# The last 64 query rows of all four experts scored as one TensorE group on four array quarters, with order and bank tables written anew

## The chip, the cores and the metric

The kernel runs on one core of a Trainium2 chip. The metric is the device time of one execution in microseconds (us). Five engines work side by side, each through its own queue in order: TensorE (PE in the profile, with PEld for its weight loads), VectorE (DVE), ScalarE (ACT), GpSimd (POOL) and SyncE (SP), which here only issues DMA transfers. Matrix products land in PSUM, which this kernel uses as eight banks of 128 partitions by 512 floats.

## The reference

Two stages follow one another for each of 8 batches of 576 rows. The first is attention with 8 heads of width 64 in which every score below (row maximum - tau) is dropped. Its output, 576 rows of 512, goes into the second stage: four experts, each a causal attention of its own with head width 64, weighted per row by a gate that keeps two of the four.

```python
scores = scale * np.matmul(q, k.transpose(0, 1, 3, 2))
scores = np.where(scores >= scores.max(-1, keepdims=True) - tau, scores, -1e9)
attn = softmax(scores); x = (attn @ v)                      # 8 batches, 8 heads, 576 x 64
...
w = softmax of the two largest of x @ w_gate
for e in range(4):                                          # second stage
    q, k, v = x @ wq[e], x @ wk[e], x @ wv[e]
    a = softmax(causal(scale * q @ k.T))
    out += w[:, :, e] * (a @ v @ wo[e])
```

## The kernel before

576 rows are four blocks of 128 and a tail of 64. The first stage takes heads in pairs (four pairs in a batch, 32 in all); the second stage takes experts in pairs (`ep` 0 and 1), the two experts `j` of a pair lying in partitions 0 to 63 and 64 to 127. `projected` makes the transposed queries and keys of a pair (tiles of the family `q2`, 128 x 576), `values` the value rows and the gate weights (`gw`, and `gt` for the tail rows). For a row block `t` of 0 to 3, `scores2` makes a score matrix per expert in a bank each, DVE adds the causal mask and takes a row minimum (L801), ACT takes the exponential with its row sum (L818), DVE inverts the sum (`inverse`: add epsilon L771, reciprocal L784), POOL multiplies by that and by the gate weight (L772). `transp2` turns the weights round on TensorE (L1355, small products with an identity, `ident`), `attnv2` multiplies by the values, and `output` by `wo` (6 products of 512 columns, `woh` and `wol`).

The tail (`t` = 4) has 64 rows for each expert, so the two experts of a pair fill one 128-partition tile together. Its scores are four products in float32: 64 query rows by 288 keys, twice, for each expert. They have a contraction of 64 and 64 result rows, so each uses one quarter of the 128 x 128 array: expert 0 the quarter (rows 0 to 63, columns 0 to 63), expert 1 the quarter (rows 64 to 127, columns 64 to 127). Both write the same bank, in different partitions. This group stands in the program twice in a batch, once for each pair. The first stage has a tail too, and scores two head pairs' tails in one group of eight such products (`kx`, `qz`): there all four quarters are in use.

The order is set by a planner (`Plan`): each step has a place (a number in the table `PLACE`, shifted by engine and tile in `PLACE_OP`), a TensorE group starts when its place comes and its tiles have room, and a table `BANKS` gives every PSUM tile its bank. `SLOTS` says how many buffers a family of tiles has. Where the planner foresees an idle TensorE in the first 160 us, `fill` puts in small products of a constant (`still`, L1352). Engines then run exactly the planned order, waiting only for data and for room.

Names in the rows: a printed name without its number is a family, so `q,q` is a product of `q2` tiles (64 x 288 is the tail, wider ones with 64*128 are the row blocks), `kx,qx` the first stage's scores, `T,vh` its products with values after a transposing DMA, `ident,p` the second stage's transposes, `pt,v` its products with values, `still` the filler. A float32 product counts as two instructions in the trace.

Of the kernel before, what the change touches and what calls it, by code (L numbers as in the profile page):

```python
# [28 lines left out]
         "x": 10, "v2": 1, "q2": 2, "zt": 2, "z0": 2, "z1": 2, "pt2": 5, "pa": 1, "pb": 2}  # L29
# [163 lines left out]
CHANGE = ((0, 160, 195, 115, 110, 160), (218, 23, 201, 119, 25, 150), (198, 163, 0, 20, 120, 163), (225, 165, 80, 0, 145, 165),  # L193
          (216, 25, 223, 150, 50, 150), (218, 150, 201, 119, 150, 23))
EXP_SB = True
AV2_GROUPS = ((4, 3), (2, 1, 0))
T2_GROUPS = ((4,), (3,), (2,), (1, 0))


# [1186 lines left out]
```

## Time and profile before

| what | value |
|---|---|
| median of 3 runs | 774.03 us (772.94 to 774.16) |
| the profiled execution | 773.78 us |
| its span, first to last instruction | 772.1 us |
| TensorE busy | 757.4 us, 98% |
| VectorE busy | 678.3 us, 88% |
| ScalarE busy | 659.3 us, 85% |
| GpSimd busy | 384.6 us, 50% |

The span leaves 1.7 us of the profiled time around it. Busy shares are averages; rows of the time line give start and length, and since TensorE's products overlap, the distance from one row's start to the next row's start is what a group really takes. The granted TensorE clock is full throughout.

### The profile page before, as it was taken

Reading aid. Unit: us, or ns where it says so; the run is one execution under the profiler, and the core shown is the slowest. Engines: PE = TensorE matmul, PEld = TensorE weight load, DVE = VectorE, ACT = ScalarE, POOL = GpSimd, SP = SyncE. Lnnn points to the kernel's source line nnn. Section 1 sums busy time; section 2 is a strip of 40 time slices with the busy share of each in tenths; the row PEclk is TensorE's granted clock in tenths of the full one; section 3 lists DMA queues with packets and bytes.
Section 4 is the critical chain, followed back from the end, with each engine's and each line's share of the span. In section 5 each row is a group of like instructions: output and inputs, shape, how many; then the busy total and the mean of one; then the engine's idle time right before and its main releaser. Section 6 shows DMA issues by size and latency. Waiting matters only on the chain.

```text
span 772.1 us, 27731 instructions
## 1 busy us (share of the span) xinstructions
PE 757.4 (98%) x10868; PEld 616.5 (80%) x10868; DVE 678.3 (88%) x2124; ACT 659.3 (85%) x1734; POOL 384.6 (50%) x547
## 2 busy tenths in 40 slices
PE   8999999999999999999999999999999999999998
PEld 6777878688777887788887887778876888778986
DVE  4899989988999889988999889998899988998374
ACT  5898879988899879988799987998899987998264
POOL 5776247543556246553475535663355633765010
PEclk9999999999999999999999999999999999999999
DMA  6541574955768577883768757696587758748002
GB/s 150 121 93 38 124 134 94 177 100 120 145 139 174 111 123 159 165 164 80 137 122 192 126 122 135 126 196 105 119 152 150 135 104 149 140 105 139 15 29 83
DMA packets 319058, 96.37 MB, mean 125 GB/s; under 512 B 305744, under 2 KB 314192, under 8 KB 318928
## 3 DMA queue, kind: packets, MB, share of 16 engines
q1 hardware_dynamic: 317584, 94.31, 61.8%
q8 instruction: 85, 1.39, 0.7%
q10 hardware_dynamic: 1344, 0.30, 0.2%
q14 instruction: 45, 0.37, 0.1%
HBM read 31.47 MB, written 9.44 MB: 53 GB/s over the span
## 4 chain that ended last, share of the span: by engine, by line
PE 68%; DVE 17%; ACT 6%; DMA 4%; issue 3%; POOL 1%; SPq 0%; ACTq 0%; DVEq 0%; POOLq 0%
PE banks L709 60%; PE banks L1355 8%; DVE pp L806 6%; DVE hl L795 3%; ACT pp L824 2%; ACT pp L818 2%; DVE col L772 2%; DMA T<-hl 2%; DMA ki<-in_k_dram 1%; DVE p L801 1%; DVE pa L746 1%; DVE st L746 1%; ACT p L818 1%; DVE x L795 1%; ACT pt L744 1%
## 5 line engine op out<-in xcount | busy, mean ns | idle before, releaser
L824 ACT ACTIVATE pp<-pp,col 128x576 f32<-128x576 f32 x284 | 209.7, 774 | 16.8 <-DVE col L784 6.1
L806 DVE TENSOR_SCALAR_CACHE_REDUCE pp<-banks 128x576 f32<-128x576 f32 x284 | 206.6, 749 | 11.7 <-PE banks L709 9.0
L772 POOL TENSOR_SCALAR hl<-pp,col 128x576 f16<-128x576 f32 x182 | 154.1, 859 | 125.9 <-DMA T<-hl 23.7
L818 ACT ACTIVATE pp<-pp 128x576 f32<-128x576 f32 x284 | 192.6, 682 | 0.1
L795 DVE SCALAR_TENSOR_TENSOR hl<-pp,col,hl 128x576 f16<-128x576 f32 x182 | 162.0, 896 | 3.3 <-POOL hl L772 3.2
L709 PE MATMUL banks<-kx,qx 64*128 64x288 f32 x1024 | 154.9, 421 | 0.9 <-ACT qz L742 0.4
L709 PEld LDWEIGHTS banks<-kx,qx 64*128 64x128 f32 x1024 | 92.3, 187 | 29.2 <-issue 6.4
L772 POOL TENSOR_SCALAR pp<-pp,col 128x576 f32<-128x576 f32 x102 | 77.2, 769 | 73.7 <-DVE col L784 37.3
L772 POOL TENSOR_SCALAR p<-p,col,gw 128x512 f32<-128x512 f32 (+3 forms) x115 | 81.1, 717 | 51.4 <-DVE col L784 40.5
L709 PEld LDWEIGHTS <-vh 128*64 128x64 f16 x2940 | 78.7, 110 | 9.5 <-issue 6.4
L709 PE MATMUL banks<-T,vh 128*64 128x128 f16 (+1 forms) x2940 | 85.1, 216 | 0.3 <-DMA T<-hl 0.2
L818 ACT ACTIVATE p<-p,col 128x512 f32<-128x512 f32 (+4 forms) x134 | 77.5, 585 | 8.3 <-DVE col L801 7.9
L801 DVE CUSTOM_DVE_ANT_0 p<-banks,mask 128x512 f32<-128x512 f32 (+4 forms) x134 | 64.3, 508 | 5.5 <-PE banks L709 5.3
L709 PE MATMUL banks<-q,q 64*64 64x288 f32 (+4 forms) x384 | 68.4, 448 | 0.1
L709 PE MATMUL banks<-wvh,x 128*128 128x260 f32 x320 | 62.5, 287 | 0.0
L744 ACT ACTIVATE pt<-banks 128x384 f32<-128x384 f32 (+2 forms) x128 | 57.6, 509 | 2.0 <-PE banks L1355 1.2
L818 ACT ACTIVATION_READ_ACCUMULATOR pp<-pp 128x1 f32 x284 | 56.7, 200 | 0.0
L709 PE MATMUL banks<-x,wqh 128*128 128x288 f32 x256 | 54.2, 304 | 0.0
L709 PEld LDWEIGHTS banks<-wvh,x 128*128 128x128 f32 x320 | 50.8, 188 | 3.8 <-issue 3.3
L709 PE MATMUL banks<-pt,v 128*64 128x128 f32 (+1 forms) x960 | 51.8, 259 | 0.4 <-ACT pt L744 0.3
L709 PE MATMUL banks<-x,wkh 128*128 128x288 f32 x256 | 52.0, 297 | 0.0
L709 PEld LDWEIGHTS banks<-pt,v 128*64 128x64 f32 x960 | 43.8, 137 | 7.3 <-issue 3.4
(141 smaller groups left out, 1553.6 us busy)
## 6 DMA issues: line engine op xcount, KB each, us to landing
ki<-in_k_dram SPq DMA_DIRECT2D x32, 256.0 KB, 3.7
vz<-in_v_dram SPq DMA_DIRECT2D x32, 256.0 KB, 2.9
qi<-in_q_dram SPq DMA_DIRECT2D x62, 128.0 KB, 2.8
out_dram<-st SPq DMA_DIRECT2D x30, 256.0 KB, 2.4
tk<-in_k_dram SPq DMA_DIRECT2D x14, 128.0 KB, 3.6
T<-hl SPq DMA_TRANSPOSE x91, 5.2
vz<-in_v_dram SPq DMA_DIRECT2D x64, 16.0 KB, 2.5
out_dram<-st SPq DMA_DIRECT2D x8, 128.0 KB, 3.3
```

Of the source, the lines that this page charges most:

```text
L709: lambda o, x, y: nc.tensor.matmul(o, x, y, start=start, stop=stop))
L744: run(e, t, [dst], [src], lambda d, s: nc.scalar.activation(d, s, AF.Copy))
L746: run(e, t, [dst], [src], lambda d, s: nc.vector.tensor_copy(d, s))
L772: return m.tensor_scalar(d, s, x_, y_, op0=op0, op1=op1)
L795: return nc.vector.scalar_tensor_tensor(d, a_, x_, r.pop(0), op0=op0, op1=op1, **kw)
L801: lambda o, a, i, m: nc.vector.tensor_tensor_reduce(o, i, m, 1.0, 3e38, ALU.add, ALU.min, a))
L806: lambda o, a, i: nc.vector.tensor_scalar(o, i, 1.0, None, op0=ALU.mult, op1=ALU.min, accum_out=a))
L818: return nc.scalar.activation(d, s, AF.Exp, scale=scale, **kw)
L824: lambda d, s, x: nc.scalar.activation(d, s, AF.Prelu, bias=x, scale=-1.0, alpha=1e36))
L1355: o.fn(*(r.place() for r in (*o.outs, *o.ins)))
```

## The change

1. `scores2` no longer handles the tail. A new `scores2_tails` scores both pairs' tails in one TensorE group of eight products. Pair 0 keeps its quarters; pair 1 is written crosswise: the product from rows 0 to 63 goes to columns 64 to 127 and the other way round. Each pair has two banks, so the group holds four.
2. Both pairs' row sums lie side by side in one small tile and are inverted by one add and one reciprocal.
3. `attnv2_tails` makes the value products of both pairs into one bank; one ACT copy and one DVE subtraction of 128 x 128 replace two each of 128 x 64.
4. Since pair 0's tail is now scored after pair 1's projections, its 64 query columns are copied by POOL into a small tile `qt`, and `q2` has three buffers in place of two.
5. `gt` is gathered crosswise. The filler constant shares its tile with `ones`.
6. `PLACE` (511 of 659 numbers), `PLACE_OP` and `BANKS` are written anew, so the order of all engines differs in many places.

```diff
-    "DVE v2": -170.4688, "DVE vh": 56.17593, "DVE warm": 30.05958, "DVE x": 53.23876, "DVE z0": 1.422731,
+    "DVE v2": -141.0707, "DVE vh": 51.88485, "DVE warm": -1.567455, "DVE x": 20.39441,
...
-         "x": 10, "v2": 1, "q2": 2, "zt": 2, "z0": 2, "z1": 2, "pt2": 5, "pa": 1, "pb": 2}
+         "x": 10, "v2": 1, "q2": 3, "zt": 2, "z0": 2, "z1": 2, "pt2": 5, "pa": 1, "pb": 2}
...
-AV2_GROUPS = ((4, 3), (2, 1, 0))
-T2_GROUPS = ((4,), (3,), (2,), (1, 0))
+AV2_GROUPS = ((3,), (2, 1, 0))
+T2_GROUPS = ((3,), (2,), (1, 0))
...
+            if not i and not ep:
+                qt = plan.tile("qt", [P, ST], F32)
+                copy("POOL", qt, t[:, SM:])
             res.append(t)
-        return res
+        return [*res, res[0][:, SM:] if ep else qt]
...
-            w = S
-            g = plan.tile("s", [P, 2, 512], F32)
-            for hf in range(2):
-                cols = slice(hf * HS, (hf + 1) * HS)
-                for rows in heads:
-                    matmul(g[rows, hf, :HS], q2[0][rows, SM:], q2[1][rows, cols], True, True, 2)
-            views = [g[:, :, :HS]]
...
+    def scores2_tails(b, q2, gates, base, pre):
+        plan.place = (base, f"{pre}s04")
+        nmx, sm = (plan.tile("col", [P, 2], F32) for _ in range(2))
+        gs = [plan.tile("s", [P, 2, 512], F32) for _ in range(EP)]
+        gs[1].v.first = gs[0].v
+        for hf in range(2):
+            cols = slice(hf * HS, (hf + 1) * HS)
+            for ep, g in enumerate(gs):
+                for j, rows in enumerate(heads):
+                    matmul(g[heads[j ^ ep], hf, :HS], q2[ep][2][rows], q2[ep][1][rows, cols], True, True)
+        p2 = []
+        for ep, g in enumerate(gs):
+            plan.place = (base, f"{pre}s{ep}4")
+            p2.append(plan.tile(("p2", "pp") if last[0] else "p2", [P, 2 * SM], F32))
+            e = halves(p2[ep][:, :S])
+            masked_min(e, g[:, :, :HS], halves(mask2), nmx[:, ep:ep + 1])
+            exp(e, e, bias=nmx[:, ep:ep + 1], accum=sm[:, ep:ep + 1], scale=-1.0)
+        inverse(sm)
+        pt = []
+        for ep, p in enumerate(p2):
+            plan.place = (base, f"{pre}s{ep}4")
+            scaled("DVE" if last[0] else "POOL", p[:, :S], p[:, :S], sm[:, ep:ep + 1], gates[1][:, ep:ep + 1], ALU.mult, ALU.mult)
...
+    def attnv2_tails(b, pt, v2, zh, zl, cols):
+        g = gbank()
+        for ep in range(EP):
+            for c in range(R + 1):
+                for j in range(2):
+                    o = c * P + (j ^ ep) * ST
+                    es = slice((2 * ep + j) * D, (2 * ep + j + 1) * D)
+                    matmul(g[heads[j], ep * ST:(ep + 1) * ST], v2[:, c, es], pt[ep][:, o:o + ST], c == 0, c == R)
+        gv = g[:, :EP * ST].rearrange("p (e c) -> p e c", e=EP)
+        copy("ACT", zh[:, :, cols], gv)
+        minus("DVE", zl[:, :, cols], gv, zh[:, :, cols].bitcast(F32))
...
+                pt = scores2_tails(b, q2, (gw, gt), base, pre)
+                if b % 2 == 0:
+                    ends[:] = [plan.tile("zt", [P, EP, P], F32R) for _ in range(2)]
+                plan.place = (base, f"{pre}a4")
+                attnv2_tails(b, pt, v2, *ends, heads[b % 2])
```

TensorE, third batch, before: pair 0's tail group (64x288 x4) ends a run of the next keys' transposes and is followed by the output of a row block.

```order
L1355 MATMUL banks<-ident,ki_61 128x64 x6
L1355 MATMUL banks<-ident,tk_86 128x64
L1355 MATMUL banks<-ident,ki_61 128x64
L709 MATMUL banks<-q_101,q_100 64x288 x4
L709 MATMUL banks<-woh,z_104 128x512
L709 MATMUL banks<-wol,z_104 128x512
```

TensorE, same batch, before: pair 1's tail group stands shortly behind the last of its projections (`x,wq`).

```order
L709 MATMUL banks<-x_94,wqh 128x288
L709 MATMUL banks<-x_93,wql 128x288
L1355 MATMUL banks<-ident,p_76 128x64 x16
L709 MATMUL banks<-kx_65,qx_63 128x288 x4
L709 MATMUL banks<-q_101,q_100 64x288 x4
```

TensorE, same batch, after: the one group of both pairs, between two outputs.

```order
L710 MATMUL banks<-wol,z_107 128x512
L710 MATMUL banks<-woh,z_108 128x512
L710 MATMUL banks<-q_100,qt_186 64x288 x2
L710 MATMUL banks<-q_101,q_102 64x288 x2
L710 MATMUL banks<-q_100,qt_186 64x288 x2
L710 MATMUL banks<-q_101,q_102 64x288 x2
L710 MATMUL banks<-woh,z_107 128x512
L710 MATMUL banks<-wol,z_107 128x512
```

Eight products stand together where four stood twice. Behind the group follow that output (six products of 512 columns), one first-stage score group (`kx,qx` 128x288 x4) and ten transposes of the next keys.

TensorE, same batch, after, right behind these: from the last of the keys' transposes to the first transposes of a tail result (`p_77`, x10).

```order
L1374 MATMUL banks<-ident,tk_85 128x64
L1374 MATMUL banks<-ident,ki_61 128x64
L710 MATMUL banks<-pt_110,v_99 64x128 x6
L710 MATMUL banks<-pt_112,v_99 64x128 x6
L710 MATMUL banks<-q_101,q_102 128x512 x2
L710 MATMUL banks<-kx_66,qx_64 128x288 x4
L1374 MATMUL banks<-ident,p_77 128x64 x10
```

Before, an output, two first-stage score groups, twelve transposes (`ident,p_76`) and one row block's scores (`q,q` 128x512 x2) stood between pair 0's group and its transposes (`ident,p_78`, x10).

POOL, third batch, before: the scaling of pair 0's tail (`p_78` with `gt`) behind two row blocks of the second stage and ahead of first-stage scalings (`hl`).

```order
L748 TENSOR_SCALAR gt_184<-gw_182 64x2 x2
L772 TENSOR_SCALAR p_76<-p_76,col_129,gw_182 128x384 x2
L772 TENSOR_SCALAR p_77<-p_77,col_119,gw_182 128x128 x2
L772 TENSOR_SCALAR p_78<-p_78,col_136,gt_184 128x576
L772 TENSOR_SCALAR hl_79<-pp_68,col_137 128x576 x2
```

POOL, same batch, after: both tails' scalings, with the same small tile `col_124` and a first-stage pair between them.

```order
L773 TENSOR_SCALAR hl_81<-pp_70,col_152 128x576 x2
L773 TENSOR_SCALAR p_77<-p_77,col_124,gt_184 128x576
L773 TENSOR_SCALAR pp_69<-pp_69,col_120 128x576 x2
L773 TENSOR_SCALAR p_76<-p_76,col_124,gt_184 128x576
L773 TENSOR_SCALAR hl_79<-pp_68,col_141 128x576 x2
```

The two tails stood nine rows apart on POOL and now stand two apart.

TensorE, last batch, after: the group stands one row of transposes behind pair 1's last key projection (`x,wk`).

```order
L710 MATMUL banks<-x_94,wkh 128x288
L710 MATMUL banks<-x_93,wkl 128x288
L1374 MATMUL banks<-ident,p_77 128x64 x12
L710 MATMUL banks<-q_100,qt_186 64x288 x2
L710 MATMUL banks<-q_102,q_101 64x288 x2
```

In the other seven batches several microseconds of TensorE work stand between them. Counted over the whole order, TensorE goes from one kind of product to another (kinds by array shape, with transposes and half-precision products apart) 531 times before and 537 times after, and has 148 fillers before and 142 after.

## Rows read from the trace of the kernel before

**Rows 1.** Page, part 1: busy us, share, instructions.

```profile
PE 757.4 (98%) x10868; PEld 616.5 (80%) x10868; DVE 678.3 (88%) x2124; ACT 659.3 (85%) x1734; POOL 384.6 (50%) x547
```

**Rows 2.** Windows: length, then busy PE, PEld, DVE, ACT, POOL, clock, DMA.

```profile
109.00:155.00 46.00, 44.88 (x668) 33.55 (x666) 44.16 (x148) 45.19 (x117) 30.31 (x39) 1.00 0.79 143
155.00:740.00 585.00, 581.64 (x8500) 475.33 (x8495) 526.59 (x1657) 512.16 (x1356) 290.84 (x397) 1.00 0.67 131
```

**Rows 3.** Windows for the filler's line alone: PE, PEld, clock, DMA.

```profile
109.00:155.00 46.00, 5.49 (x37) 2.96 (x37) 1.00 0.79 143
```

**Rows 4.** Groups of TensorE products, shapes apart: count, busy us, mean ns, idle before.

```profile
L709 PE MATMUL banks<-kx,qz 64*64 64x288 f32 x256 | 19.3, 415 | 0.0
L709 PE MATMUL banks<-q,q 64*64 64x288 f32 x128 | 19.0, 415 | 0.0
```

**Rows 5.** Time line of TensorE around pair 0's tail group, third batch: start, length.

```profile
288.12 0.35 PE L1355 MATMUL banks<-ident,ki 64*128 64x64 f32 x6
...
288.31 0.22 PE L1355 MATMUL banks<-ident,ki 64*128 64x64 f32 x1
288.47 1.19 PE L709 MATMUL banks<-q,q 64*64 64x288 f32 x8
289.59 0.50 PE L709 MATMUL banks<-woh,z 128*128 128x512 f32 x1
```

**Rows 6.** Time line of TensorE around a first-stage tail group on four quarters.

```profile
227.74 1.20 PE L709 MATMUL banks<-kx,qz 64*64 64x288 f32 x16
228.87 0.28 PE L709 MATMUL banks<-col,ones 128*64 128x1 f32 x4
229.08 0.50 PE L709 MATMUL banks<-woh,z 128*128 128x512 f32 x1
...
230.67 1.24 PE L709 MATMUL banks<-kx,qx 64*128 64x288 f32 x8
231.84 0.50 PE L709 MATMUL banks<-woh,z 128*128 128x512 f32 x1
```

**Rows 7.** Time line, all engines: the way of that tail from exponential to transposes.

```profile
290.88 0.77 ACT L818 ACTIVATE p<-p,col 128x576 f32<-128x576 f32 x1
291.55 0.20 ACT L818 ACTIVATION_READ_ACCUMULATOR p<-p,col 128x1 f32 x1
291.88 2.17 POOL L772 TENSOR_SCALAR p<-p,col,gw 128x384 f32<-128x384 f32 x4
292.07 0.17 DVE L784 RECIPROCAL col<-col 128x1 f32<-128x1 f32 x1
293.95 1.13 PE L709 MATMUL banks<-q,q 64*128 64x512 f32 x4
294.02 0.83 POOL L772 TENSOR_SCALAR p<-p,col,gt 128x576 f32<-128x576 f32 x1
294.91 0.52 PE L1355 MATMUL banks<-ident,p 64*128 64x64 f32 x10
```

**Rows 8.** Time line of TensorE, last batch: value products of 128 columns.

```profile
755.87 2.84 PE L709 MATMUL banks<-pt,v 128*64 128x128 f32 x48
```

**Rows 9.** Time line, last batch: last product of a projection and its copy.

```profile
746.32 0.29 PE L709 MATMUL banks<-x,wql 128*128 128x288 f32 x1
746.71 0.41 ACT L744 ACTIVATE q<-banks 128x288 f32<-128x288 f32 x1 [1.25 <-PE banks L709]
```

**Rows 10.** Groups of DVE and POOL instructions that the change adds or removes.

```profile
L755 DVE TENSOR_TENSOR zt<-banks,zt 128x64 fp32r<-128x64 f32 x16 | 3.4, 212 | 1.4 <-ACT zt L744 1.2
L755 DVE TENSOR_TENSOR z<-banks,z 128x128 fp32r<-128x128 f32 x16 | 4.5, 284 | 3.1 <-ACT z L744 3.1
L784 DVE RECIPROCAL col<-col 128x1 f32<-128x1 f32 x16 | 2.5, 156 | 0.2
L772 POOL TENSOR_SCALAR p<-p,col,gw 128x128 f32<-128x128 f32 x28 | 13.0, 473 | 5.7 <-ACT zt L744 3.0 <-ACT x L742 1.6 <-DVE col L772 1.0
```

**Rows 11.** Waits: POOL for a reciprocal; total us, times, longest.

```profile
POOL hl L772 <- DVE col L784: 20.5, 13, 2.7
```

More of the change, by code (lines that the diff above doesn't have):

```diff
@@ L160 @@
-    "ACT wqh": -8.614884, "ACT wvh": -61.59402, "ACT x": 51.80171, "ACT z0": 13.77228, "ACT z1": 21.38886,
-    "ACT zt": 75.06289, "DVE col": -65.78447, "DVE gate": -58.83315, "DVE gt": 50.60351, "DVE gw": -85.47739,
-    "DVE hl": 114.5464, "DVE kx": -5.703491, "DVE lg": 91.45051, "DVE p2": -17.02737, "DVE pa": 5.055651,
-    "DVE pp": 1.799467, "DVE qsc": 151.7334, "DVE st": 9.31911, "DVE still": -70.95507, "DVE tau_p": -59.16886,
-    "DVE v2": -170.4688, "DVE vh": 56.17593, "DVE warm": 30.05958, "DVE x": 53.23876, "DVE z0": 1.422731,
@@ L170 @@
-    "POOL woh": 39.26528, "POOL wol": 61.43774, "POOL wqh": 90.91714, "POOL wql": -33.05171, "POOL wvh": -25.50643,
-    "POOL wvl": -100.8319, "SP T": -284.0837, "SP ki": -32.54941, "SP lg": -23.16328, "SP out": -197.8732,
-    "SP qi": 0.244049, "SP st": -150.7584, "SP tk": 9.732419, "SP tq": -143.6642, "SP vz0": -34.81607,
-    "SP vz1": -20.35572,
+    "ACT gw": -162.6874, "ACT kx": 108.3985, "ACT lg": 32.86921, "ACT p2": -218.0769, "ACT pb": -180.7968,
+    "ACT pp": 93.41855, "ACT pt2": -44.22563, "ACT q2": -81.22372, "ACT q2d0": -19.04289, "ACT q2d1": -63.05565,
@@ new lines @@
+    "ACT qi": 97.04683, "ACT qx": -46.61529, "ACT qz0": -36.58193, "ACT qz1": -122.443, "ACT tau_t": 22.37296,
+    "ACT tq": 88.41551, "ACT v2": 14.9347, "ACT warm": 82.36406, "ACT wkh": 33.61568, "ACT woh": -31.10502,
+    "ACT wqh": -8.614884, "ACT wvh": -61.59402, "ACT x": 66.07489, "ACT z0": 71.76126, "ACT z1": 35.58804,
+    "ACT zt": 67.6444, "DVE col": -83.97126, "DVE gate": -92.70674, "DVE gt": 104.5688, "DVE gw": -39.35556,
+    "DVE hl": 136.2087, "DVE kx": 3.353303, "DVE lg": 91.45051, "DVE ones": 31.69671, "DVE p2": 5.73354,
@@ new lines @@
+    "DVE pa": 8.331859, "DVE pp": 7.85189, "DVE qsc": 77.806, "DVE st": 5.74597, "DVE still": -44.37944,
+    "DVE tau_p": -47.34204, "DVE v2": -141.0707, "DVE vh": 51.88485, "DVE warm": -1.567455, "DVE x": 20.39441,
+    "DVE z0": 6.209092, "DVE z1": 44.79113, "DVE zt": 21.07184, "POOL col": -52.95213, "POOL gate": 27.92703,
+    "POOL gt": -49.52221, "POOL gw": 18.22398, "POOL hl": 107.7234, "POOL ident": 34.97707, "POOL mask": 185.7308,
+    "POOL mask2": -70.88285, "POOL ones": -68.97509, "POOL p2": 22.65193, "POOL pp": -67.71528, "POOL q2d0": 82.12945,
@@ new lines @@
+    "POOL q2d1": -277.5747, "POOL qt": -40.16381, "POOL qz0": -58.87586, "POOL qz1": -44.37684, "POOL st": 46.66943,
+    "POOL tie": -21.55509, "POOL v2": 2.057049, "POOL vh": -69.38473, "POOL vz0": 60.40645, "POOL vz1": -49.95888,
+    "POOL wkh": -62.83705, "POOL wkl": 10.16045, "POOL woh": 63.31141, "POOL wol": 62.66516, "POOL wqh": 70.22473,
+    "POOL wql": -18.89272, "POOL wvh": 14.14287, "POOL wvl": -96.68153, "SP T": -235.5178, "SP ki": -2.032985,
+    "SP lg": -17.05672, "SP out": -200.5112, "SP qi": 11.85062, "SP st": -168.3793, "SP tk": -44.33728,
@@ L849 @@
     qsc = const("qsc", [P, 1])
-    still = const("still", [P, P], BF16)
-    memset("DVE", still, 1.0)
+    ones = const("ones", [P, D])
+    memset("DVE", ones, 1.0)
+    still = ones.bitcast(BF16)
     memset("DVE", warm, 0.0)
@@ L873 @@
         memset("POOL", t[:, 2 * R * D:], 0.0)
-    memset("POOL", ones, 1.0)
     heads = [slice(j * D, (j + 1) * D) for j in range(2)]
@@ L1198, in values @@
         gt = plan.tile("gt", [P, EP], F32)
-        for j in range(2):
-            copy(soft, gt[j * ST:(j + 1) * ST], gw[ST:, R, j::2])
+        copy(soft, gt[:ST], gw[ST:, R, ::E - 1])
+        copy(soft, gt[ST:], gw[ST:, R, 1:E - 1])
         return v2, gw, gt
@@ L1205, in scores2 @@
         nmx, sm = (plan.tile("col", [P, 2], F32) for _ in range(2))
-        if t < R:
-            w = (t + 1) * P
-            gs = [gbank()[:, :w] for _ in range(2)]
-            gs[1].v.first = gs[0].v
-            for g, rows in zip(gs, heads):
-                matmul(g, q2[0][rows, t * P:w], q2[1][rows, :w], True, True)
-            views = gs
-        else:
-            w = S
-            g = plan.tile("s", [P, 2, 512], F32)
-            for hf in range(2):
-                cols = slice(hf * HS, (hf + 1) * HS)
-                for rows in heads:
-                    matmul(g[rows, hf, :HS], q2[0][rows, SM:], q2[1][rows, cols], True, True, 2)
-            views = [g[:, :, :HS]]
+        w = (t + 1) * P
+        views = [gbank()[:, :w] for _ in range(2)]
+        views[1].v.first = views[0].v
+        for g, rows in zip(views, heads):
+            matmul(g, q2[0][rows, t * P:w], q2[1][rows, :w], True, True)
         p2 = plan.tile(("p2", "pp") if last[0] else "p2", [P, 2 * SM], F32)
         for j, sv in enumerate(views):
-            e = p2[:, j * SM:j * SM + w] if t < R else halves(p2[:, :S])
-            masked_min(e, sv, mask[:, SM - w:] if t < R else halves(mask2), nmx[:, j:j + 1])
+            e = p2[:, j * SM:j * SM + w]
+            masked_min(e, sv, mask[:, SM - w:], nmx[:, j:j + 1])
             exp(e, e, bias=nmx[:, j:j + 1], accum=sm[:, j:j + 1], scale=-1.0)
-        nj = len(views)
         gw, gt = gates
-        inverse(sm[:, :nj])
-        gg = gw[:, t, 2 * ep:2 * ep + 2] if t < R else gt[:, ep:ep + 1]
-        for j in range(nj):
+        inverse(sm)
+        gg = gw[:, t, 2 * ep:2 * ep + 2]
+        for j in range(2):
             p = p2[:, j * SM:j * SM + w]
@@ L1233, in scores2 @@
         return p2
+    def scores2_tails(b, q2, gates, base, pre):
[15 more added lines that the diff above has]
+            exp(e, e, bias=nmx[:, ep:ep + 1], accum=sm[:, ep:ep + 1], scale=-1.0)
+        inverse(sm)
+        pt = []
+        for ep, p in enumerate(p2):
+            plan.place = (base, f"{pre}s{ep}4")
+            scaled("DVE" if last[0] else "POOL", p[:, :S], p[:, :S], sm[:, ep:ep + 1], gates[1][:, ep:ep + 1], ALU.mult, ALU.mult)
+            plan.place = (base, f"{pre}t{ep}4")
+            blocks = [(p[:, c * P:(c + 1) * P],) * 2 for c in range(R)] + [(p[:, S - P:S],) * 2]
+            pt.append(blocks_out(blocks, plan.tile("pt2", [P, len(blocks) * P], F32)))
+        return pt
+    def attnv2_tails(b, pt, v2, zh, zl, cols):
+        g = gbank()
+        for ep in range(EP):
+            for c in range(R + 1):
+                for j in range(2):
+                    o = c * P + (j ^ ep) * ST
[4 more added lines that the diff above has]
+        minus("DVE", zl[:, :, cols], gv, zh[:, :, cols].bitcast(F32))
     def transp2(tiles, p2, base, name):
@@ L1257, in attnv2 @@
                     es = slice((2 * ep + j) * D, (2 * ep + j + 1) * D)
-                    if t < R:
-                        x = pts[:, (j * (t + 1) + c) * P:(j * (t + 1) + c + 1) * P]
-                    else:
-                        x = pts[:, c * P + j * ST:c * P + (j + 1) * ST]
+                    x = pts[:, (j * (t + 1) + c) * P:(j * (t + 1) + c + 1) * P]
                     matmul(g[j * D:(j + 1) * D, o:o + m], v2[:, c, es], x, c == 0, c == t)
             o += m
-        a = 0
-        while a < o:
-            zh, zl, cols = z[tiles[0] if a == 0 else R - 1]
-            m = cols.stop - cols.start
-            copy("ACT", zh[:, ep, cols], g[:, a:a + m])
-            minus("DVE", zl[:, ep, cols], g[:, a:a + m], zh[:, ep, cols].bitcast(F32))
-            a += m
+        zh, zl, cols = z[tiles[0]]
+        copy("ACT", zh[:, ep, cols], g[:, :o])
+        minus("DVE", zl[:, ep, cols], g[:, :o], zh[:, ep, cols].bitcast(F32))
     def output(b, t, zh, zl, cols):
@@ L1292 @@
     family("gt", EP, 2)
+    family("qt", ST, 1)
     ends = []
@@ L1303, in moe @@
         v2, gw, gt = values(b, base, pre, parts)
-        tiles = (4, 3, 2, 1, 0)
+        tiles = (3, 2, 1, 0)
         for ep in range(EP):
@@ L1307, in moe @@
                 q2[1] = projected(b, 1, base, pre)
+                pt = scores2_tails(b, q2, (gw, gt), base, pre)
[3 more added lines that the diff above has]
+                attnv2_tails(b, pt, v2, *ends, heads[b % 2])
+                if b % 2:
+                    plan.place = (base, f"{'LM' if b == B - 2 else pre}o{R}")
+                    output(b, R, *ends, slice(0, P))
             pts, p2 = {}, {}
@@ L1317, in moe @@
                     if ep == 0:
-                        for x in ts:
-                            if x == R:
-                                if b % 2 == 0:
-                                    ends[:] = [plan.tile("zt", [P, EP, P], F32R) for _ in range(2)]
-                                z[x] = *ends, heads[b % 2]
-                            elif x == ts[0] or x == R - 1:
-                                zs = [plan.tile(f"z{k_}", [P, EP, words[f"z{k_}"] // EP], F32R) for _ in range(2)]
-                                z[x] = *zs, slice(0, words[f"z{k_}"] // EP)
+                        zs = [plan.tile(f"z{k_}", [P, EP, words[f"z{k_}"] // EP], F32R) for _ in range(2)]
+                        z[ts[0]] = *zs, slice(0, words[f"z{k_}"] // EP)
                     plan.place = (base, f"{pre}a{ep}{k_}")
```

48 lines of the change are left out of this document (16 added, 32 removed), and 236 rows, old and new, of the table PLACE.

## The prediction

> **What bounds the kernel now.** The first view is the page's busy shares: TensorE 98%, DVE 88%, ACT 85%, POOL 50% [rows 1]. An average over a long run can hide stages with other limits, so the second view is the table of windows [rows 2]. From 155 to 740 us, more than six of the eight batches, TensorE is busy for 581.64 of 585 us while DVE has 58 us free and ACT 73: there the time is the sum of what TensorE does, and a microsecond taken out of its work is a microsecond off the end unless a wait takes its place. Ahead of it, from 109 to 155 us, where the first batch's second stage starts, DVE and ACT are as full as TensorE (44.16 and 45.19 of 46 us), and 37 of TensorE's instructions are fillers [rows 3]: TensorE waits there, and less work for it is worth little. The third view is the time line, in which one reads the distance from start to start, since lengths of neighbouring rows overlap.
>
> **What the change takes from TensorE.** The trace holds both forms of a tail group. Sixteen second-stage groups on two quarters cost 19.0 us together, that is 1.19 us each; sixteen first-stage groups with twice the products on four quarters cost 19.3 us, 1.21 us each [rows 4]. So eight products on four quarters take as long as four on two. From start to start the first is 288.47 to 289.59 = 1.12 us [rows 5] and the second 227.74 to 228.87 = 1.13 us [rows 6]. The change runs 8 groups where 16 stood: 8 x 1.12 = **-8.96 us**. The group that is left is taken at 1.13 as before; crosswise quarters with two banks for each pair are not in the trace in just this form, and if they did not overlap the group would take 2 x 1.12 and nothing would be gained. I take the lower end because the four quarters themselves, in another pairing with banks, are there at 1.13.
>
> A page speaks against this. The rows: in the group of rows 5 both halves of the array's rows write one bank, in different partitions, and four products take 1.12 us, no more than four first-stage products that write two separate banks (230.67 to 231.84 = 1.17 us) [rows 6]. The Trainium skill, "TensorEngine Tiling (Array Packing)", Gotcha 1: PSUM Pressure, says that different row tiles cannot access the same bank at the same time. By that rule the group of rows 5 should take about double; the trace disagrees. In the changed group each pair's bank is again written from both row halves, so by the rule the sum would be 0 instead of -8.96; it is the second rival below.
>
> **Switches.** Going from one kind of product to another costs time of its own. In rows 5 six transposes take 288.12 to 288.31, 0.03 us each, but the last one's start lies 0.16 us ahead of the group's: about 0.13 us for the switch. The order after has 537 switches for 531. The distance of 1.12 us already holds the switch out of a group, so of the 8 removed groups 8 switches are paid for and 14 more come in elsewhere. Many of those are between transposes and other products with 64 rows, of which I have no clean row, so a price between 0 and 0.13 us: 0 to 1.8 us; I take 0.05, **+0.7 us**.
>
> **First and last batch.** In the first batch the group that goes away stands among fillers [rows 3], so most of its 1.12 us is not won. What DVE and ACT lose there counts instead, and it is small. DVE gives up two 212 ns subtractions for one of 284, and two reciprocals of 156 ns with the adds ahead of them for one of each [rows 10]: 0.14 + 0.3 = about 0.4 us a batch. That leaves **+0.7 us** of the 1.12 to be given back (between 0 and 1.1). In the last batch the group stands 12 transposes behind pair 1's last key projection. Such a projection ended at 746.61 and its ACT copy at 747.12, 0.51 us later [rows 9]; 12 transposes at 0.03 are about 0.4: **+0.1 us** once. In the other batches microseconds stand between, before as after.
>
> **Costed at nothing.** The saved ACT and DVE work in the other batches: both have over 50 us free there [rows 2]. The `qt` copy on POOL, 128 x 64: a 128 x 128 scaling took 473 ns [rows 10], so at most 0.5 us a batch on an engine that is half idle; if POOL were late already, it would cost the same 0.5 x 7 = 3.5 us. Four banks at once for the group: the first stage's tail group holds as many and shows no idle time ahead of it [rows 4]. The third `q2` buffer can only bring projections forward. SP's output transfers of the tail rows move with their group; SP waits for data, not data for it.
>
> **The wait that is added.** Both tails' sums go through one reciprocal, so the first tail's scaling on POOL now waits for the second tail's exponential. Behind it in POOL's queue stand a first-stage scaling pair, the second tail and a further `hl` pair whose transposing DMA feeds TensorE. Before, the way was: group over at 289.59, exponential at 290.88 (0.77 + 0.20 us), reciprocal done at 292.24, but POOL at the other scalings from 291.88 and at this one from 294.02 to 294.85; TensorE began its transposes at 294.91 without idling [rows 5, 7]. So 5.26 us from group to scaled tile, with 5.32 us of TensorE work in between: no slack to speak of. After, one exponential more: 5.26 + 0.97 = 6.23 us. The work in between is now an output (229.08 to 230.67 = 1.59), two score groups (2 x 1.17) [rows 6], the keys' transposes (about 0.4) [rows 5], 12 value products, 24 instructions (2.84 / 2 = 1.42 less the overlap, 1.4) [rows 8], and one row block's scores (293.95 to 294.91 = 0.96) [rows 7]: 6.7 us. So 0.47 us to spare: **0 us**, from 0 to what the rivals say.
>
> **Sum.** -8.96 + 0.7 + 0.7 + 0.1 = -7.46 us on the profiled execution's own 773.78 us gives 766.3; the median of the runs shown lies 0.25 us higher, so **766.6 us**.
>
> **Rivals.** *First, POOL late in part.* All places are new, and in the new order the first-stage scalings that stand ahead of the first tail on POOL themselves wait for reciprocals: such waits were 20.5 us in 13 times, 1.58 us in the mean, 2.7 at the longest [rows 11]. A mean wait in half of seven batches makes 6.23 + 1.58 - 6.7 = 1.1 us x 3.5 = 3.9 us: 770.5 us. For it: before had no slack at all. Against it: TensorE idled only 3.4 us in 585 [rows 2], so such waits fell mostly where they cost nothing. *Second, the quarters do not overlap crosswise*, so the change doesn't do what it says: the group takes 2.24 us, nothing is won, and with 0.7 for switches the time is 774.0 + 0.7 = about 774.7 us (same). Against it: rows 5 and 6, as above. *Third, slower:* POOL's first tail scaling comes late by the longest wait, 2.7 us, in every batch. The place is the transposes of the first tail; 6.23 + 2.7 - 6.7 = 2.2 us x 7 = 15.6 us are lost against 7.46 won: 782 us. It decides from the point where the scaled tile ends more than 6.7 + 1.1 = 7.8 us after its group, for then each batch gives back its whole gain. For it: DVE and ACT are 90 and 88% busy in that stretch, and every reciprocal goes through DVE's queue. Against it: the order has moved everything, and nothing says that this queue was forgotten.
>
> **How the numbers follow.** A measurement of this kernel tells about 0.2% from no change, 1.5 us; faster means below 772.5. The forecast (762 to 769) has 0.64, POOL late in part (769 to 772.4) 0.15, no overlap or a wait that eats the gain up (772.5 to 775.6) 0.09, slower 0.12. Faster is 0.64 + 0.15 = 0.79. The lower end of the range is 774.03 - 8.96 with batch one's relief in DVE and fewer idle stretches (up to 3 us of the 3.4 left in rows 2): 762; the upper end takes in the first rival and the beginning of the next, 773.5. About 0.2 is left out.
>
> **What would show it.** Right: one row of 16 instructions of the tail form per batch, about 1.2 us long, 9.6 us for all eight; TensorE busy some 8 us less; idle time between 155 and 735 us still 3 to 4 us. The switches show as a busy time that falls by less than 9. Wrong in the first step: tail groups of 2.2 us. Wrong in the wait: idle TensorE time ahead of the first transposes of a tail, with POOL as the releaser. If TensorE's idle time rises elsewhere, the new order and not the group has decided.

## The result: 10 us slower

The changed kernel takes 783.97 us (median of 4 runs, 783.19 to 784.44) where the kernel before, on the same chip, takes 773.73: ratio 1.0132, 95% interval 1.0115 to 1.0150. The prediction was 766.6 with a range to 773.5. The profiled execution is of 784.44 us, its span 782.7.

The page of the changed kernel: busy us, share and instructions, then the start of the chain that ended last; below it that chain in the kernel before.

```profile
PE 756.6 (97%) x10862; PEld 620.1 (79%) x10862; DVE 683.2 (87%) x2100; ACT 663.7 (85%) x1726; POOL 395.8 (51%) x554
...
PE 51%; DVE 30%; ACT 9%; issue 5%; DMA 2%; SPq 1%; POOL 1%; POOLq 0%; DVEq 0%; ACTq 0%
```

```profile
PE 68%; DVE 17%; ACT 6%; DMA 4%; issue 3%; POOL 1%; SPq 0%; ACTq 0%; DVEq 0%; POOLq 0%
```

Against [rows 1], TensorE's busy time fell by 0.8 us and not by some 8, and its idle time rose from 14.7 to 26.1 us. In the kernel before, DVE held 17% of the chain, now it holds 30%.

The tail groups did what was foreseen. Groups of TensorE products of the changed kernel (count, busy us, mean ns, idle before):

```profile
L710 PE MATMUL banks<-q,q 64*64 64x288 f32 x64 | 9.5, 415 | 0.0
L710 PE MATMUL banks<-q,qt 64*64 64x288 f32 x64 | 9.5, 415 | 0.4 <-DVE pp L807 0.4
```

Where [rows 4] had 128 instructions in 19.0 us, two halves of 64 now run in the same 9.5 us. Third batch, time line of TensorE (start, length; in brackets idle time ahead and its releaser), first a place some 10 us ahead of the group, then the group:

```profile
312.26 1.24 PE L710 MATMUL banks<-kx,qx 64*128 64x288 f32 x8
...
313.72 0.22 PE L1374 MATMUL banks<-ident,ki 64*128 64x64 f32 x1
314.61 1.24 PE L710 MATMUL banks<-kx,qx 64*128 64x288 f32 x8 [0.67 <-DVE pp L807]
...
322.00 0.46 PE L710 MATMUL banks<-q,qt 64*64 64x288 f32 x2
322.01 0.46 PE L710 MATMUL banks<-q,q 64*64 64x288 f32 x2
...
323.13 0.50 PE L710 MATMUL banks<-woh,z 128*128 128x512 f32 x1
```

The two pairs start 0.01 us apart, and from start to start the group takes 322.00 to 323.13 = 1.13 us. The loss shows in the rows above it. Two groups of first-stage scores (`kx,qx`, four PSUM banks each) stand only the keys' transposes apart. By the program's table the first takes banks 1, 2, 4 and 5 and the second 0, 1, 2 and 3, while the transposes between them fill 6 and 7. So the second takes two banks of the first again, and it waits 0.67 us for one that DVE has not read out. DVE at that time, columns alike:

```profile
312.17 0.79 DVE L796 SCALAR_TENSOR_TENSOR hl<-pp,col,hl 128x576 f16<-128x576 f32 x1
...
313.09 0.79 DVE L796 SCALAR_TENSOR_TENSOR hl<-pp,col,hl 128x576 f16<-128x576 f32 x1
313.81 0.74 DVE L807 TENSOR_SCALAR_CACHE_REDUCE pp<-banks 128x576 f32<-128x576 f32 x1
314.48 0.07 DVE L807 DVE_READ_ACCUMULATOR pp<-banks 128x1 f32 x1
```

The reading-out of the score banks (L807) stands in DVE's queue behind two subtractions for the first stage (L796), and TensorE goes on 0.06 us after it. The same two score groups in the kernel before:

```profile
307.38 1.19 PE L709 MATMUL banks<-kx,qx 64*128 64x288 f32 x8
308.51 1.19 PE L709 MATMUL banks<-q,q 64*64 64x288 f32 x8
309.63 2.82 PE L709 MATMUL banks<-T,vh 128*64 128x64 f16 x120
...
314.73 1.24 PE L709 MATMUL banks<-kx,qx 64*128 64x288 f32 x8
```

There pair 1's tail group, value products, transposes and an output, 7.35 us from start to start, gave DVE time; now it is 2.35 with the wait. The distance alone is not the measure. Two other score groups of the first stage, the same two before and after:

```profile
200.81 2.21 PE L709 MATMUL banks<-kx,qx 64*128 64x288 f32 x16
202.99 0.59 PE L1355 MATMUL banks<-ident,p 64*128 64x64 f32 x12
```

```profile
204.91 1.24 PE L710 MATMUL banks<-kx,qx 64*128 64x288 f32 x8
205.98 0.60 PE L710 MATMUL banks<-q,q 64*128 64x256 f32 x4
207.00 1.24 PE L710 MATMUL banks<-kx,qx 64*128 64x288 f32 x8 [0.42 <-DVE pp L807]
```

Before, the two stand back to back, 2.18 us for both, on eight different banks, and TensorE does not wait. After, they are 2.09 us apart, share banks 2 and 3, and the second waits. What counts is whether the banks that a group takes have been read out.

All waits for `pp` readings in the changed kernel (us, times, longest; PE the products, PEld their weight loads), and the largest group of products in both kernels, changed and before:

```profile
PE banks L710 <- DVE pp L807: 6.4, 14, 0.9
PEld banks L710 <- DVE pp L807: 12.5, 21, 1.2
```

```profile
L710 PE MATMUL banks<-kx,qx 64*128 64x288 f32 x1024 | 161.9, 423 | 9.4 <-DVE pp L807 5.7 <-DVE x L756 1.3 <-ACT pt L745 1.2
```

```profile
L709 PE MATMUL banks<-kx,qx 64*128 64x288 f32 x1024 | 154.9, 421 | 0.9 <-ACT qz L742 0.4 <-ACT pb L744 0.2 <-DVE pp L806 0.2
```

The same 1024 instructions are busy 7.0 us longer (mostly stalls inside a group, which count as busy) with 8.5 us more of idle time ahead: that alone is more than the eight groups save. When each wait over 0.1 us is matched to the bank that ended it, TensorE waits for a late bank 37 times, 13.4 us in all, and 15 times, 4.5 us, in the kernel before.

Last, windows over the five batches from the third's first key transposes to the eighth's (length, then busy PE, PEld, DVE, ACT, POOL), changed and before. They hold five periods of the order, so what stands at their ends does not matter:

```profile
139.23:604.53 465.30, 454.15 (x6661) 371.99 (x6663) 424.01 (x1306) 417.29 (x1081) 247.82 (x328) 1.00 0.69 136
```

```profile
143.42:599.65 456.23, 453.39 (x6630) 367.74 (x6630) 421.68 (x1319) 411.21 (x1082) 233.88 (x321) 1.00 0.71 138
```

Five groups fewer should make 456.23 - 5.6 = 450.6 us; it is 465.3. **So 14.7 of the 19.6 us that are missing** (782.7 against 772.1 - 9.0) **are lost in these five batches**, 4.9 at the start and in the last batch. TensorE's idle time in the five batches rose by 8.3 us, and its busy time, with five groups fewer, by 0.8. DVE still has 41 of 465 us free there: on the average it is not short of time, but late in places.

A part of the 14.7 us is not the order's directly. A window of the changed kernel, columns alike, the granted clock being the third number from the end:

```profile
148.33:151.74 3.41, 3.32 (x30) 1.82 (x32) 0.68 (x3) 2.09 (x6) 3.00 (x5) 0.50 0.92 173
```

For 3.4 us the granted clock was 0.50, the lower level of 1.2 GHz, as a wait ended in which TensorE had stood idle for 1.94 us (its row stands below, under the first batch). At half speed that costs this execution up to 1.7 us. In the kernel before the clock was full in both stretches of [rows 2].

### The profile page after: what moved, and what is told of

Read it like the earlier page. It is cut to its first block, busy times and chain, and to the rows that moved or that the text cites. A ratio compares the mean times of both kernels' runs of the same rounds, so it can differ in the third digit from the quotient of the medians.

```text
span 782.7 us, 27639 instructions
## 1 busy us (share of the span) xinstructions
PE 756.6 (97%) x10862; PEld 620.1 (79%) x10862; DVE 683.2 (87%) x2100; ACT 663.7 (85%) x1726; POOL 395.8 (51%) x554
## 4 chain that ended last, share of the span: by engine, by line
PE 51%; DVE 30%; ACT 9%; issue 5%; DMA 2%; SPq 1%; POOL 1%; POOLq 0%; DVEq 0%; ACTq 0%
PE banks L710 45%; DVE pp L807 8%; DVE hl L796 6%; PE banks L1374 6%; DVE col L773 3%; ACT pp L825 3%; ACT pp L819 3%; DVE p L802 3%; DVE pt L747 2%; DMA T<-hl 1%; DVE st L747 1%; DVE pa L747 1%; DVE col L772 1%; SPq L835 1%; ACT p L819 1%
## 5 line engine op out<-in xcount | busy, mean ns | idle before, releaser
L807 DVE TENSOR_SCALAR_CACHE_REDUCE pp<-banks 128x576 f32<-128x576 f32 x284 | 209.3, 747 | 7.7 <-PE banks L710 6.5
L710 PE MATMUL banks<-kx,qx 64*128 64x288 f32 x1024 | 161.9, 423 | 9.4 <-DVE pp L807 5.7
L796 DVE SCALAR_TENSOR_TENSOR hl<-pp,col,hl 128x576 f16<-128x576 f32 x182 | 160.2, 889 | 6.0 <-POOL hl L773 5.9
L710 PEld LDWEIGHTS banks<-kx,qx 64*128 64x128 f32 x1024 | 95.7, 186 | 45.1 <-DVE pp L807 11.0
L773 POOL TENSOR_SCALAR p<-p,col,gw 128x384 f32<-128x384 f32 (+3 forms) x117 | 90.1, 778 | 51.3 <-DVE col L785 13.5
L819 ACT ACTIVATE p<-p,col 128x384 f32<-128x384 f32 (+4 forms) x138 | 79.8, 583 | 13.7 <-DVE col L802 13.2
L802 DVE CUSTOM_DVE_ANT_0 p<-banks,mask 128x384 f32<-128x384 f32 (+4 forms) x138 | 66.4, 510 | 9.1 <-PE banks L710 8.8
L710 PE MATMUL banks<-q,q 64*128 64x128 f32 (+4 forms) x320 | 59.9, 458 | 0.1
```

What stands on the lines that cost most here:

```text
L710: lambda o, x, y: nc.tensor.matmul(o, x, y, start=start, stop=stop))
L773: return m.tensor_scalar(d, s, x_, y_, op0=op0, op1=op1)
L796: return nc.vector.scalar_tensor_tensor(d, a_, x_, r.pop(0), op0=op0, op1=op1, **kw)
L802: lambda o, a, i, m: nc.vector.tensor_tensor_reduce(o, i, m, 1.0, 3e38, ALU.add, ALU.min, a))
L807: lambda o, a, i: nc.vector.tensor_scalar(o, i, 1.0, None, op0=ALU.mult, op1=ALU.min, accum_out=a))
L819: return nc.scalar.activation(d, s, AF.Exp, scale=scale, **kw)
```

## The experiments

**Are the crosswise quarters worth their 9 us?** The order and the banks stay, the second pair takes the same quarters as the first:

```diff
-                    matmul(g[heads[j ^ ep], hf, :HS], q2[ep][2][rows], q2[ep][1][rows, cols], True, True)
+                    matmul(g[heads[j], hf, :HS], q2[ep][2][rows], q2[ep][1][rows, cols], True, True)
```

> The changed kernel, instruction for instruction in the same order and banks, but pair 1's tail is written straight and not crosswise, so that both pairs use the same two quarters of the array (the gate weights of the tail are gathered to match). Theory A (the group is worth what was forecast and the order loses more): the group takes 2.2 us and the time rises by 6 to 9 us, to 790 to 793. Theory C (the group's gain is swallowed where it stands by waits right behind it): the group takes 2.2 us, but the time stays within 2 us of 784. If the quarters never overlapped crosswise, nothing changes at all, group length included.

Measured: 787.02 us (785.55 to 787.64), 3.0 above the changed kernel, between the two theories. (On the chip of this run and of the next two the kernel before took 774.76, 1.0 more than above, so 2 to 3 us.) Its time line of TensorE, third batch:

```profile
320.05 0.70 PE L710 MATMUL banks<-q,qt 64*64 64x288 f32 x4
320.59 0.65 PE L710 MATMUL banks<-q,q 64*64 64x288 f32 x4
321.07 0.65 PE L710 MATMUL banks<-q,qt 64*64 64x288 f32 x4
321.56 0.65 PE L710 MATMUL banks<-q,q 64*64 64x288 f32 x4
322.14 0.50 PE L710 MATMUL banks<-woh,z 128*128 128x512 f32 x1
```

Straight, the group takes 2.09 us, so crosswise saves 0.96 in each, 7.7 in eight; 2 to 3 of them reach the end. With TensorE's products as long as in the kernel before, the new order is 12 to 13 us slower: the cost is the order's, and it swallows most of what the quarters give.

**Is it the new table of banks?** First the banks of both kernels by a rule, the order untouched: each tile gets the banks with the widest gap to their uses before and after, in the planner's times.

```diff
-        for v, x in zip(tiles, BANKS):
-            v.slot = self.families[v.fams[0]][DIGITS.index(x)]
+        for v in sorted(tiles, key=lambda v: v.span):
+            got = [(space(v, s), -i, s) for i, s in enumerate(self.families[v.fams[0]])]
+            v.slot = max([x for x in got if x[0] is not None], key=lambda x: x[:2])[2]
```

> The kernel before with its order untouched and its table of banks replaced by a rule: every PSUM tile gets the bank that leaves the widest planned gap to its neighbours there. All theories expect about the time of before, 773.7 us, within 3 us; it shows what the rule itself costs or gains, so that the same edit on the changed kernel can be read.

> The changed kernel with its order untouched and its new table of banks replaced by the same widest-gap rule. Theory B (the new banks make TensorE wait for banks that DVE has not yet read): at least half of the 10 us come back, 779 us or less. Theory A (the new order of DVE, ACT and POOL makes TensorE wait, whatever the bank): 784 us, within 2 us of the changed kernel, corrected by what the rule does to the kernel before.

Measured: 792.32 us (792.23 to 792.48) for the kernel before, 808.67 (806.75 to 810.97) for the changed one. 18 and 25 us from a table alone was expected by nobody, and the traces say why. The kernel before with the rule, around a tail group, TensorE and then DVE:

```profile
409.38 1.19 PE L715 MATMUL banks<-q,q 64*64 64x288 f32 x8
410.50 0.44 PE L715 MATMUL banks<-T,vh 128*64 128x64 f16 x16
411.91 2.56 PE L715 MATMUL banks<-T,vh 128*64 128x64 f16 x104 [0.97 <-DVE col L807]
```

```profile
411.09 0.76 DVE L807 CUSTOM_DVE_ANT_0 p<-banks,mask 128x576 f32<-128x576 f32 x1 [0.17 <-PE banks L715]
411.77 0.08 DVE L807 DVE_READ_ACCUMULATOR2_ANT col<- 128x1 f32 x1
```

By the program's allotment the value products go to bank 5 and do not need the scores; the scores lie in banks 4 and 6. DVE reads both with one instruction, a view with a step, and TensorE stands still until it ends. The program's dependencies take such a view for the whole stretch from the first bank to the last. Of the waits over 0.1 us, 24 with 19.2 us end right behind the read of a pair that lies across the wanted bank, in the changed kernel with the rule 30 with 29.6 us; in the two kernels as they were, none and one of 0.1. So both tables avoid it, and the rule does not speak on theory B. A second table does, chosen by the times of the changed kernel's own trace and with that cost counted:

```diff
 BANKS = (
-    "03122046206464744571074233207302461616144232326744532763236702066046720163067362325454062026202431304517016075"
...
```

> Changed kernel, every instruction in its order, but another table of banks, chosen by the times of the changed kernel's own trace: a bank that was read out longest before TensorE wants it, and never a bank that lies between the two banks of a pair that VectorE still has to read. In the changed kernel's trace TensorE waits 13.4 us in 37 places for a bank that is read out late (before: 4.5 us in 15). Theory A (the late reader is the cause, and all eight banks are in use wherever TensorE waits): the best table that the search found takes at most 4 us off these waits, so 780 to 784. Theory B (the new table of banks is the cause): 772 to 777.

Measured: 784.26 us (783.01 to 785.96). TensorE's idle time fell from 26.1 to 22.3 us, but its busy time rose from 756.6 to 761.9. The pair of score groups shown above, with this table:

```profile
204.37 1.24 PE L710 MATMUL banks<-kx,qx 64*128 64x288 f32 x8
205.44 0.60 PE L710 MATMUL banks<-q,q 64*128 64x256 f32 x4
205.88 1.82 PE L710 MATMUL banks<-kx,qx 64*128 64x288 f32 x8
```

The wait ahead of the second group is gone and stands inside it: 1.82 us instead of 1.24. So another table, chosen with care, wins nothing; that no table could help this order is not shown.

**Is it DVE's lateness?** VectorE gets less to do, in both kernels, with the order and the banks as they are. This and the later reliefs, but for the scaling by ScalarE, leave a part of the computation out; they only show who waits for whom.

```diff
             stt(hl[:, 1, at], pp[:, at], ss[:, h:h + 1], hl[:, 0, at], ALU.mult, ALU.subtract)
+            if n >= 2 * NPAIR:
+                full = plan.ops[-1].fn
+                plan.ops[-1].fn = lambda *r, full=full: full(*(x[:, :HS] if x.shape[-1] == S else x for x in r))
```

> Changed kernel, same order and banks, but from the third batch's pairs on VectorE's subtraction that makes the low halves (hl) covers 288 of its 576 columns, the rest is left as it is: about 0.4 us off each of some 150 instructions, so VectorE has 60 us less to do in the run; TensorE's work is unchanged. Theory A (in the new order VectorE reads the score banks out late, and TensorE waits for them): the waits behind the first 160 us go, 784 falls by 8 to 12 us to 772 to 776, and below the kernel before. Theory B (TensorE's waits have another cause, banks or ScalarE or GpSimd): 781 to 784.

> The control of the run above: the kernel before with the same half subtraction from the third batch's pairs on. Theory A (there VectorE's reading is hidden behind TensorE): 772 to 774, under 2 us gained. Theory B (VectorE's lateness sets the end in both kernels alike): 764 to 768.

Measured: 772.25 us (771.16 to 773.85) and 769.77 (769.67 to 770.32). The same 42 to 47 us off DVE bring the changed kernel 11.7 us and the kernel before 3.9, twice what was expected of the control. Theory A holds in the main: 7.8 us of the gain exist only in the new order. The control's 3.9 lie between its two theories: VectorE was not wholly hidden before. But the changed kernel does not come out 9 us below the control, it stays 2.5 above.

**GpSimd and ScalarE.** The tails' scaling on 64 of 576 columns, in both kernels:

```diff
             scaled("DVE" if last[0] else "POOL", p[:, :S], p[:, :S], sm[:, ep:ep + 1], gates[1][:, ep:ep + 1], ALU.mult, ALU.mult)
+            full = plan.ops[-1].fn
+            plan.ops[-1].fn = lambda *r, full=full: full(*(x[:, :D] if x.shape[-1] == S else x for x in r))
```

> Changed kernel, same order and banks, but the scaling of the sixteen scored tails (GpSimd's, and VectorE's in the last batch) covers 64 of 576 columns: GpSimd has some 14 us less to do, 0.9 us less in each place. Theory A (VectorE is late by the order of its own work): 782 to 784. Theory C (GpSimd's scaling, which took 1172 ns instead of 811, and beside which VectorE's instructions are stretched, holds up the tail and VectorE): 775 to 779.

> Control of the run that cut the changed kernel's tail scaling to 64 of 576 columns (778.2 against 784): the same cut in the kernel before. Theory A (GpSimd's scaling does its harm through VectorE, which only the new order makes late): 772.5 to 774, at most 1 us gained. Theory C (the scaling holds up any order): 766 to 770.

Measured: 778.23 us (777.77 to 779.06), 5.7 gained, and 773.10 (772.58 to 774.79), 0.6 gained. (The 1172 ns of the expectation are those of the 512-column scaling; the tails' own went from 850 to 1040.) Scaling by ScalarE instead:

```diff
+            if not last[0]:
+                def scale(d, s_, x, y):
+                    nc.vector.tensor_tensor(x, x, y, op=ALU.mult)
+                    return nc.scalar.activation(d, s_, AF.Copy, scale=x)
+                plan.ops[-1].fn = scale
```

> Changed kernel, same order and banks, and the whole computation: in all batches but the last the tails are scaled by ScalarE instead of GpSimd, at the same place of the program, after VectorE has multiplied reciprocal and gate (14 small instructions). GpSimd has 16 us less to do, ScalarE some 8 us more. Theory A (GpSimd's scaling costs by what it does to VectorE, and ScalarE has room): 778 to 781. Rival (ScalarE, 85% busy, takes the place of GpSimd as the late one): 784 to 788.

Measured: 784.62 us (784.15 to 786.19), nothing gained, as the rival said. DVE's busy time fell to 679.0 us, as in the run with the cut (679.1, from 683.2), and that alone brought nothing. But ScalarE had 7.5 us more to do (671.2 from 663.7), so whether less stretching of DVE beside GpSimd is a part of what the cut gained is not shown. And ScalarE relieved:

```diff
             kinked(c, c, thr[:, j:j + 1])
+            if n >= 2 * NPAIR:
+                full = plan.ops[-1].fn
+                plan.ops[-1].fn = lambda d, s_, x, full=full: full(d[:, :1], s_[:, :1], x)
```

> Changed kernel, same order and banks, but from the third batch's pairs on ScalarE's first pass over the first stage's scores (the kinked one, L825) covers 288 of 576 columns, the rest goes on as it is: about 0.24 us off each of some 250 instructions, 60 us off ScalarE, as much as the half subtraction took off VectorE. Theory A (VectorE's own queue is what runs late, ScalarE is only along the way): 779 to 783. Theory D (ScalarE is as late as VectorE, and VectorE waits for it): 771 to 775.

Measured: 779.71 us (778.16 to 782.48), 4.3 gained for 41 us off ScalarE, where the same off VectorE brought 11.7. VectorE matters most. This relief alone was not run in the kernel before, so how much of the 4.3 the change brought is not shown.

**Is that all?** The straight group with VectorE relieved, then all three reliefs at once (VectorE's from the sixth pair on, ScalarE's in all pairs, the tails' scaling) in the changed kernel, the kernel before and the straight one:

> The changed kernel with VectorE's half subtraction (772.3) and the second pair's halves put straight, on the same quarters as the first pair's, so that TensorE's tail group takes 2.2 us and not 1.1, eight times 1.1 us more. With VectorE in full the same edit cost 3.0 us. Theory A (TensorE waits for VectorE swallow what TensorE saves; relieved of that, the quarters are worth what they save): 777.5 to 780.5. Rival (the quarters are worth 3 us whatever VectorE does): 774.5 to 776.

> Changed kernel, same order and banks, three engines relieved at once: VectorE's half subtraction from the sixth pair on, ScalarE's half first pass (L825) in all pairs, the tails' scaling on 64 of 576 columns. TensorE's work is whole. Theory A (the whole loss is TensorE waiting for the three engines in the new order): TensorE is the bound again and the eight groups' 9 us are there, 758 to 763. Rival E (a part of the loss is in TensorE's own new order, which no relief of the others takes away): 766 to 770.

> The control: the kernel before with the same three reliefs. Both theories: TensorE was the bound and still is, 767 to 770.

> The changed kernel with the three reliefs and the second pair straight, so that each of the eight groups takes 2.1 us and not 1.1. Theory A: 7.5 to 9 us above the same kernel crosswise, level with the kernel before with the reliefs (766 to 771). Rival E: 3 to 5 us above the same kernel crosswise, as with VectorE relieved alone.

Measured: straight with VectorE relieved 776.43 us (775.92 to 777.69), 4.2 above the crosswise and between the theories; with all reliefs changed 766.43 (765.73 to 768.20), before 768.32 (767.82 to 769.18), straight 772.06 (769.56 to 773.12). The three reliefs bring the changed kernel 17.5 us and the kernel before 5.4. The 12.1 between them are the part of the missing 19.2 us (10.2 slower and 9.0 not won) that hangs on the three engines in the new order. The changed kernel is now 1.9 us below the control and not 9: the total is in rival E's range, though whether the rest lies in TensorE's own order, as E says, is not shown. Windows over the same five batches, columns as above, relieved: changed, before, straight.

```profile
140.83:592.32 451.49, 446.52 (x6663) 368.61 (x6663) 379.32 (x1306) 382.22 (x1083) 221.40 (x328) 1.00 0.71 140
```

```profile
142.25:594.95 452.70, 450.19 (x6630) 365.93 (x6630) 380.09 (x1320) 378.75 (x1083) 212.13 (x322) 1.00 0.72 140
```

```profile
138.87:595.28 456.41, 451.52 (x6666) 370.60 (x6664) 381.87 (x1306) 382.89 (x1083) 221.44 (x328) 1.00 0.71 140
```

In these executions straight costs 4.92 us more than crosswise in five groups, 0.98 each, as much as the groups' lengths say; by the medians, over executions up to 3.6 us apart, it is 5.6 in eight groups, 0.70 each, between theory A and the rival. Without reliefs the windows are 465.87 straight and 465.30 crosswise, the second with up to 1.7 us lost by the clock, so 0.1 to 0.5 each. So the quarters are worth the more, the less TensorE waits for the others: 2 to 3, 4.2 and 5.6 us of the 7.7.

Against the control the changed kernel should be 5.6 us below in the five batches and is 1.2 below: 4.4 stay of the 14.7 us, or of 13.0 without the clock. At the start and in the last batch 4.9 us were lost, and with the reliefs it is 766.5 - 451.49 against 766.1 - 452.70 less 3.4 for three groups, 5.0. But there the clock fell at the start, behind a wait of 1.5 us:

```profile
21.55:24.97 3.42, 3.42 (x30) 2.29 (x29) 0.00 (x0) 2.90 (x8) 2.16 (x4) 0.50 0.67 139
```

That again is up to 1.7 us, so 3.3 to 5.0 stay.

What makes these 4.4 and 3.3 to 5.0 is left open. A part is seen. With all reliefs TensorE waits 9.1 us for late banks in the whole run (2.8 in the control). In the five batches alone these waits are left, and the control has none of them:

```profile
PE banks L710 <- DVE pp L807: 2.4, 6, 0.4
PE banks L710 <- ACT pt L745: 1.0, 3, 0.3
```

A score group 2 us behind another takes some of its banks again, and DVE needs 1.5 us to read out four, however little else it has to do.

## Why the prediction was wrong

**The group** (-8.96 us) was right: 1.13 us in place of 2 x 1.12 (1.33 in the first batch alone), and crosswise quarters overlap, so the second rival did not happen; straight quarters did what it describes, 2.09 us. Two row halves again write one bank at the same time.

**The wait that is added** came out right in its size. Third batch, GpSimd's scaling of the two tails and TensorE's transposes of the first:

```profile
328.13 1.24 POOL L773 TENSOR_SCALAR p<-p,col,gt 128x576 f32<-128x576 f32 x1 [1.00 <-DVE col L785]
...
330.80 0.82 POOL L773 TENSOR_SCALAR p<-p,col,gt 128x576 f32<-128x576 f32 x1
```

```profile
329.59 0.90 PE L1374 MATMUL banks<-ident,p 64*128 64x64 f32 x10
```

From the group's end at 323.13 to the scaled tile at 329.37 it is 6.24 us; the prediction said 6.23. That close it is by luck: the prediction had POOL busy with other scalings and a scaling of 0.83 us, but POOL waited 1.00 us for the reciprocal and scaled for 1.24. The transposes follow 0.2 us later without idling. In the six middle batches the way takes 5.6 to 6.3 us, so the third rival's price is not paid in any of them.

**First batch** (+0.7) was wrong: here POOL was late and TensorE idle for it, as in the first and third rivals, but not for a reciprocal. POOL, then TensorE:

```profile
145.75 0.74 POOL L773 TENSOR_SCALAR hl<-pp,col 128x576 f16<-128x576 f32 x1 [1.15 <-DMA T<-hl]
146.48 1.88 POOL L773 TENSOR_SCALAR p<-p,col,gt 128x576 f32<-128x576 f32 x1
```

```profile
148.42 0.80 PE L1374 MATMUL banks<-ident,p 64*128 64x64 f32 x10 [1.94 <-POOL p L773]
```

The group had ended at 139.15, so this tail took 9.2 us, over the 7.8 from which the prediction saw a batch's whole gain given back. POOL had waited for a DMA to free an `hl` tile, and the scaling took 1.88 us. The window of 109 to 155 us that [rows 2] shows now reads:

```profile
109.00:155.00 46.00, 41.17 (x622) 30.85 (x622) 40.48 (x126) 41.15 (x102) 25.21 (x35) 0.96 0.72 132
155.00:740.00 585.00, 574.27 (x8524) 474.09 (x8520) 527.79 (x1620) 515.35 (x1344) 305.75 (x407) 1.00 0.67 131
```

TensorE is idle for 4.8 us there (before 1.1), and the granted clock is 0.96 by the fall shown above. **Switches** and **last batch** cannot be read apart from waits.

**Costed at nothing** is the step that failed. The prediction took the time as the sum of TensorE's work plus the one wait behind the group. The new order of all engines stands in its sum only as 14 switches, and DVE's 58 and ACT's 73 us of free time in 585 [rows 2] were taken to cover the rest. The second line shows the same 57 us of DVE free, and TensorE idle for 7.4 more. That free time was an average. What the runs showed in its place: in the new order TensorE waits for banks that DVE, and less often ACT, have not read out, 22 times and 8.9 us more than before, mostly ahead of first-stage scores, which the change does not name, and more stalls stand inside the groups. Of the missing 19.2 us 12.1 hang on DVE, ACT and POOL, 7.8 of them on DVE's subtractions alone; the other 7.1 are open. A change that writes every place anew need not keep the places where a reading-out had time, and the prediction gave that case no price: its slower rival put 0.12 on one wait behind the group. Its last sentence, that idle time elsewhere means that the order has decided, is what happened. The Trainium skill, "Perfetto Trace Analysis", Optimizing Tensor Performance, advises to rotate product groups through banks so that the reading-out of one overlaps the next; the traces agree: two score groups back to back on eight different banks did not wait, and two that were 2.09 us apart and shared two banks waited 0.42.

## What to carry to other kernels

A saving on the engine that is busy 98% is only as good as the order around it: if a change re-lays the order, follow for each group that fills PSUM which banks it takes and when the reading engine will have emptied them, in its queue and not on the average. To tell a late helper from other causes, halve a part of its work in both kernels with the order frozen; the difference of the two gains (11.7 against 3.9 us) exists only in the new order. And price an order that is new throughout as a risk of its own.

## Not expected

A pair of PSUM banks that is read through a stepped view blocks the banks between the two for the length of the read, by the program's dependencies and not by the chip: 24 waits, 19.2 us in one kernel, 0.97 us in the rows shown. GpSimd's scaling of the tails cut by 0.43 us in each of 14 places brought 5.7 us in the changed kernel; why so much is not settled.
